# A planner for TensorE's order that counts changes of matmul shape and tends to keep a shape, with the remainders of the MLP's first level put last

## The chip, the core and the metric

The kernel runs on one NeuronCore of a Trainium2 chip. The metric is device time in microseconds (us) of the whole program, as the median of several runs. A profile of one execution stands beside it; its span runs from the first to the last instruction.

## The reference

Two blocks follow each other. The first is a recurrence over 768 steps for 4 batches and 8 heads, with a state of 40 x 40 for each:

```python
for t in range(S):
    y[:, :, t] = np.einsum('bhd,bhde->bhe', rt, state)
    Sa = np.einsum('bhde,bhe->bhd', state, at)
    state_decay = state * wt[:, :, None, :] - np.einsum('bhd,bhe->bhde', Sa, bt)
    state = state_decay + np.einsum('bhd,bhe->bhde', vt, kt)
```

Its output, brought into the form of 3072 tokens x 320, goes through an MLP with a hidden width of 2048, all in fp32:

```python
h = x @ w_in
g = h * (1.0 / (1.0 + np.exp(-h)))
return (g @ w_out).astype(np.float32)
```

## The kernel before

**The work.** The 768 steps are cut into 12 chunks of 64. Within a chunk the recurrence becomes matrix products: products between the scaled keys and the a vectors (between(), L560), the inverse of a unit triangular 64 x 64 matrix for each of 32 problems, a solve, and reads and updates of the state. Each chunk's output of 320 x 256 is then the input of the MLP for its 256 tokens.

For chunk n the following steps run, each written as a planned operation on one engine:

- load(n) and load_r(n) issue DMAs on SP: the decay w into wz, then b and k into kbv, a, v into vu, r and v transposed.
- prepare(n): VectorE scans the decays down and up (L505, L523), POOL (VectorE for n < 4) multiplies b and k into kb (L542) and scales a (L532). TensorE makes the products with b and with k (L560), the product with v (sv, L621) and two transposes of kb into kt (L646). ACT evicts (L633, L659, L285), VectorE masks (L606).
- special(n) for the chunks below NS = 4: a 16 x 16 inverse on VectorE with transfers through DRAM, and three steps on TensorE (L790, L803, L835, summed by VectorE in L850).
- inverse(k) for each pair of chunks from 4 on: the blocks of both chunks go through DRAM into mi, VectorE inverts 32 x 32 blocks (multiply L672, reduce L673), and DMAs bring the blocks into ZQ and X. merge(n) joins them with two groups of small matmuls (L915, L944).
- chain(n): the state is applied to a (right, L987, summed with R in L997), the solve (L1011) with its eviction into vu (L285, L289), its transposed form (solve_t, L1042), the transpose of the state G into GT (L1072), the update of the state (L1099, then L1115 on VectorE).
- read(n): products of r with v and u (look, L1141, masked in L1153) and then write(): the state's part (L1178) and the part of the chunk (L1191), both accumulated in one PSUM tile. VectorE scales it (L1202); it goes to DRAM (xh, L1219) and bring(n) fetches it as xt (L1259, L1261).
- moe(n): the MLP. The first level multiplies w_in by xt: 320 rows are two full tiles of 128 rows (full, L1271) and a remainder of 64 rows (rest, L1284), in which two row halves are used. Four rooms of 4 x 256 columns each are filled; the order is full(0), rest(0 and 1), full(1), then the same for 2 and 3. ACT applies the activation (gate, L1294). The second level (second, L1311) accumulates 16 matmuls with w_out for each of two halves of 128 tokens, VectorE copies the result (L1323) and SP sends it out.

**PSUM.** Four tiles called pair, of two banks each, hold all matmul results. A Room is a claim on one of them: it is taken by the first operation that names it and given back after a stated number of operations. Two more tiles, lam, in SBUF, are shared in the same way.

**The order.** No order is written out. Every step calls add(engine, cost, do, reads, writes, pri, rooms, k): the cost in us, a priority in which 10 stands for a chunk, and the number of instructions k that TensorE has to fetch. Plan.order() simulates five engines: for each engine it looks at the operations that are ready, takes those that can start within SLACK of the earliest (0.4 us for TensorE), and of these the one with the smallest priority. Among the engines it takes the operation that starts first. walk() models the fetching of TensorE's instructions in blocks of 256, and MOST and SHARE keep small matmuls (k over 32) and large ones (k of 32 or less) mixed. The operations are then issued in this order, which is fixed when the program is built: each engine works its queue in order and waits by semaphores. A cost in the planner changes no duration on the chip, only the order. `ahead()` lowers the priority value by 9 for the steps of chain, read and bring that are not on TensorE.

```python
least = min(x for _, x, _ in starts)
near = [x for x in starts if x[1] <= least + self.SLACK[e]]
if e == "PE" and mixed > self.MOST:
    near = [x for x in near if x[2]["k"] < 33] or near
s, _, op = min(near, key=lambda x: (x[2]["pri"], x[2]["n"]))
```

Of the kernel before, what the change touches and what calls it, by code (L numbers as in the profile page):

```python
# [32 lines left out]
class Plan:  # L33
# [8 lines left out]
    def add(self, engine, cost, do, r=(), w=(), pri=0, rooms=(), k=0, size=0.0, after=0.0):  # L42
        op = dict(
            engine=engine, cost=cost, do=do, pri=pri, rooms=rooms, k=k, size=size, n=len(self.ops), after=after
        )
# [21 lines left out]
    MOST, SHARE = 1.5, 2.0  # L67

# [24 lines left out]
    def order(self):  # L93
        ops = self.ops
        self.fetched, self.count = [0.0, 0.0], 0
# [9 lines left out]
        for op in ops:  # L105
            op["ready"] = op["after"]
        while len(out) < len(ops):
            best = None
            for e, some in ready.items():
                starts = []  # L110
                for op in some:
# [7 lines left out]
                    if e == "PE" and s < 1e8:  # L119
                        lost = self.walk(s, op["cost"], op["k"]) - s - op["cost"]  # L120
# [7 lines left out]
                s, _, op = min(near, key=lambda x: (x[2]["pri"], x[2]["n"]))  # L128
# [8 lines left out]
            at[e] = end = self.walk(s, op["cost"], op["k"], True) if e == "PE" else s + op["cost"]  # L137
# [29 lines left out]
def kernel(  # L167
# [171 lines left out]
    def weights(n):  # L339
# [42 lines left out]
        for h in range(2):  # L382
            for i in (1, 0):
# [10 lines left out]
                add("PE", 0.97, sum_, me, [(pf, h)], pri, [pf], 2)  # L394
# [93 lines left out]
    def prepare(n):  # L488
# [80 lines left out]
        add("PE", 1.14, partial(between, 1, pb_), ["B", ("a", i3)], [pb_, ("sb", i2)], pri, [pb_], 128)  # L569
# [17 lines left out]
        else:  # L587
            for b in range(2):
                for c in range(2):
                    q0 = 64 * i2 + 32 * c + 16 * b  # L590
                    r0 = 64 * b + 32 * c
                    dma(
                        lambda q0=q0, r0=r0, c=c: nc.sync.dma_start(
                            md[n // 2 % 2][q0 : q0 + 16].rearrange("q s t -> s q t"),
# [4 lines left out]
                        [("md", n // 2 % 2, i2, b, c)],  # L599
# [3 lines left out]
        add("PE", 1.14, partial(between, 0, pk), ["K", ("a", i3)], [pk], pri + 0.5, [pk, sk], 128)  # L603
# [25 lines left out]
        add("PE", 1.14, sv, [sk, ("v", i2, 0), ("v", i2, 1)], [pv, ("R", i3)], pri + 0.6, [pv, sk], 128)  # L629
# [9 lines left out]
        for b in range(2):  # L639
# [15 lines left out]
            add("PE", 0.75, turn, ["K", "B"], [pt, ("kt", i3, b)], pri + 0.7, [pt], 33)  # L655
# [76 lines left out]
    def special(n):  # L732
# [82 lines left out]
        for part in parts:  # L815
            XI_, X_ = keyed(("XI",), part), keyed(("X2", i2), part)
            k = len(part)
            add("PE", 0.57 * k, partial(both, pm[part], lambda b, g: S_[half(b), g, :], block, part), [("sb", i2), *mik], [pm[part], *XI_], pri, [pm[part]], 64 * k)
            add("PE", 0.3 * k, partial(turn, pd[part], part), mik, [pd[part]], pri, [pd[part]], 16 * k)
# [706 lines left out]
```

## Time and profile before

| what | value |
|---|---|
| median of 3 runs | 751.06 us (749.36 to 753.55) |
| the profiled execution | 748.01 us, with a span of 746.2 us |
| mean granted TensorE clock | 0.987 |
| VectorE / ACT / POOL busy | 53% / 26% / 11% of the span |
| first matmul | 13.71 us after the start |
| mean share of DMA engines, moved | 75.72 MB in the span |

The page's groups name a line, an engine, an operation, output and inputs, the shape and the count; then busy time, mean duration in ns, and the idle time of the engine just ahead of it with the releaser. PE is TensorE's matmul, PEld its weight load, which overlaps it. An fp32 matmul appears as two passes, so that 32 matmuls of one planned operation give 64 entries. The ends of matmuls are modelled and overlap the next start; the time of a group is therefore taken here from its start to the start of the group after it.

### The profile page before, as it was taken

To read this page: it belongs to the slowest core of one execution; us is meant where nothing else is said; L and a number is where in the kernel's file an instruction comes from. 1 tells how busy PE (TensorE), PEld (TensorE's weight loads), DVE (VectorE), ACT (ScalarE), POOL (GpSimd) and SP (SyncE) were. 2 spreads that over 40 slices of the span, in tenths; PEclk is the share of its full clock that TensorE was granted. 3 is DMA by queue.
4 is the path that set the end of the run, shared out by engine and by line. 5 is a ranking of instruction groups with operands and counts; after the bars stand their busy time and mean duration, and the time that the engine had idled before them with its cause. 6 is when DMAs were issued, how large, how long until landed. Compare 5 with 4: busy or idle time off the path is not lost.

```text
span 746.2 us, 27622 instructions
## 1 busy us (share of the span) xinstructions
PE 680.2 (91%) x12810; PEld 538.4 (72%) x12810; DVE 397.0 (53%) x567; ACT 195.9 (26%) x240; POOL 81.9 (11%) x63
## 2 busy tenths in 40 slices
PE   2198998999979999999998999998999999999995
PEld 2176786687768777787776777776777878778773
DVE  6867889674624298245496344496354293320000
ACT  3264355032223113313213213213213203111010
POOL 3200000003004003103220013130013000000000
PEclk9999998999999999999999999999999999999999
DMA  7672833561532343354532344432341404121000
GB/s 246 154 231 74 273 123 94 155 183 19 144 88 87 96 124 79 92 136 125 135 94 70 64 121 131 133 94 66 69 117 44 111 18 87 42 63 40 18 1 22
DMA packets 116956, 75.72 MB, mean 101 GB/s; under 512 B 64546, under 2 KB 113634, under 8 KB 116194
## 3 DMA queue, kind: packets, MB, share of 16 engines
q1 hardware_dynamic: 112328, 63.10, 32.1%
q0 software_dynamic: 2096, 10.49, 4.0%
q8 instruction: 102, 1.67, 1.0%
q10 hardware_dynamic: 2410, 0.30, 0.3%
q14 instruction: 20, 0.16, 0.1%
HBM read 59.64 MB, written 13.83 MB: 98 GB/s over the span
## 4 chain that ended last, share of the span: by engine, by line
PE 64%; DVE 19%; DMA 6%; issue 3%; SPq 2%; ACT 2%; POOL 2%; ACTq 1%; DVEq 0%; POOLq 0%
PE pair L1311 21%; PE pair L1271 15%; DVE XI L672 6%; PE pair L1284 4%; DVE XI L673 4%; DMA wz<-in_wT 3%; PE pair L835 3%; PE pair L1141 3%; PE pair L1191 3%; DVE kbv L505 2%; PE pair L560 2%; PE pair L1099 2%; DVE wz L523 2%; POOL kb L542 2%; PE pair L1178 2%
## 5 line engine op out<-in xcount | busy, mean ns | idle before, releaser
L1311 PE MATMUL pair<-wo,gts 128*128 128x320 f32 x768 | 225.2, 445 | 2.5 <-ACT kt L659 2.5
L1311 PEld LDWEIGHTS pair<-wo,gts 128*128 128x128 f32 x768 | 143.6, 192 | 59.2 <-ACT kt L659 2.7
L1271 PE MATMUL pair<-xt,wi 128*128 128x256 f32 x768 | 179.5, 388 | 4.4 <-DMA xt<-xh 2.3
L1271 PEld LDWEIGHTS pair<-xt,wi 128*128 128x128 f32 x768 | 144.2, 192 | 29.5 <-issue 4.0
L1294 ACT ACTIVATE gts<-pair 128x1024 f32<-128x1024 f32 x48 | 49.1, 1023 | 178.2 <-PE pair L1271 92.1
L542 POOL TENSOR_TENSOR kb<-kbv 128x512 f32<-128x512 f32 (+1 forms) x24 | 48.3, 2028 | 321.8 <-DVE wc L512 220.6
L560 PE MATMUL pair<-a,kb 40*64 40x64 f32 x1536 | 30.2, 236 | 28.8 <-DVE a L532 28.8
L560 PEld LDWEIGHTS pair<-a,kb 40*64 40x64 f32 x1536 | 27.5, 149 | 34.0 <-issue 18.6
L1284 PE MATMUL pair<-xt,wi 64*128 64x256 f32 x384 | 48.9, 391 | 3.0 <-DVE ot L1323 2.0
L1323 DVE COPY ot<-pair 128x320 f32<-128x320 f32 x24 | 11.7, 488 | 70.5 <-PE pair L1311 70.5
L673 DVE TENSOR_REDUCE XI<-XI 128x64 f32<-128x512 f32 (+9 forms) x68 | 46.9, 690 | 2.3
L1284 PEld LDWEIGHTS pair<-xt,wi 64*128 64x128 f32 x384 | 35.0, 186 | 12.2 <-issue 5.4
L1153 DVE TENSOR_TENSOR lam<-pair,ml 128x1024 f32<-128x1024 f32 x24 | 29.0, 1219 | 23.8 <-PE pair L1141 23.8
L672 DVE TENSOR_TENSOR XI<-XI,mi 128x1024 f32<-128x1024 f32 (+8 forms) x48 | 36.2, 754 | 5.8 <-DMA mi<-md 4.7
L1202 DVE TENSOR_TENSOR lam<-pair,wz 128x1024 f32<-128x1024 f32 (+1 forms) x13 | 14.8, 1142 | 45.9 <-PE pair L1191 45.7
L523 DVE TENSOR_TENSOR_SCAN wz<-wz,zt 128x1024 f32<-128x1024 f32 x12 | 31.6, 2631 | 0.4
L1141 PEld LDWEIGHTS pair<-r,vut 40*64 40x64 f32 x1536 | 24.8, 135 | 6.1 <-issue 5.6
L606 DVE TENSOR_TENSOR lam<-pair,ml 128x1024 f32<-128x1024 f32 x12 | 14.6, 1219 | 27.2 <-PE pair L560 23.9
L1141 PE MATMUL pair<-r,vut 40*64 40x64 f32 x1536 | 27.9, 221 | 0.9 <-issue 0.9
L505 DVE TENSOR_TENSOR_SCAN kbv<-wz,zt 128x1024 f32<-128x1024 f32 x12 | 27.5, 2291 | 1.0
L1085 ACT COPY GT<-pair 128x640 f32<-128x640 f32 x11 | 7.6, 692 | 75.1 <-PE pair L1072 75.1
L285 ACT ACTIVATE sb<-pair 128x1024 f32<-128x1024 f32 x12 | 12.3, 1023 | 56.8 <-PE pair L560 56.8
(146 smaller groups left out, 725.9 us busy)
## 6 DMA issues: line engine op xcount, KB each, us to landing
wz<-in_wT SPq DMA_DIRECT2D x12, 512.0 KB, 5.2
kbv<-in_bT SPq DMA_DIRECT2D x12, 512.0 KB, 3.7
a<-in_aT SPq DMA_DIRECT2D x12, 512.0 KB, 5.3
kbv<-in_kT SPq DMA_DIRECT2D x12, 512.0 KB, 4.8
r<-in_rT SPq DMA_DIRECT2D x48, 96.0 KB, 2.6
vut<-in_vT SPq DMA_DIRECT2D x48, 96.0 KB, 3.1
vu<-in_v SPq DMA_DIRECT2D x24, 160.0 KB, 4.0
out<-ot SPq DMA_DIRECT2D x48, 80.0 KB, 2.0
```

The source lines that it names most:

```text
L505: nc.vector.tensor_tensor_scan(back(V), back(W[:, 2 : 2 + Q * C]), zt, 1.0, ALU.mult, ALU.add)
L523: nc.vector.tensor_tensor_scan(Z, Z, zt, 0.0, ALU.mult, ALU.add)
L542: TTn[engine].tensor_tensor(out=at_(kb, place(is_b, first), (576 * step, 4 // step), (128, 4), (1, C)), in0=blocks((kf, bf)[is_b]), in1=bl ...
L560: nc.tensor.matmul(room.tile[half(b), j, g * C : g * C + C], lhsT=kb[rows(j), place(is_b, q) : place(is_b, q) + C], rhs=A[rows(j), q * C : ...
L672: nc.vector.tensor_tensor(out=at_(tmp, 0, *dims), in0=x, in1=y, op=ALU.mult)
L673: nc.vector.tensor_reduce(out=out_, in_=at_(tmp, 0, *dims), axis=AX.X, op=ALU.add)
L1141: nc.tensor.matmul(pl.tile[half(1 - b if role else b), b, c * C : c * C + C], lhsT=vut[rows(b), role, hu, :], rhs=rs[rows(b), hh, :], star ...
L1153: lambda pl=pl, la=la: nc.vector.tensor_tensor(out=la.tile.rearrange("p (q t) -> p q t", q=Q), in0=pl.tile.rearrange("p a b -> p (a b)").r ...
L1271: nc.tensor.matmul(rooms[g].tile[:, f // 2, (f % 2) * T : (f % 2) * T + T], lhsT=wi[:, k, (4 * g + f) * 128 : (4 * g + f) * 128 + 128], rh ...
L1284: nc.tensor.matmul(rooms[g].tile[:, h, (f % 2) * T : (f % 2) * T + T], lhsT=wi3[half(h), g * 256 + (f % 2) * 128 : g * 256 + (f % 2) * 128 ...
L1294: nc.scalar.activation(out=gts[:, 4 * g * T : 4 * g * T + 4 * T], in_=rooms[g].tile.rearrange("p a b -> p (a b)"), func=AF.Silu)
L1311: nc.tensor.matmul(po[b].tile[:, 0, 0:DM], lhsT=g4[:, f, 128 * b : 128 * b + 128], rhs=wo[:, f, :], start=f == 0, stop=f == NF - 1,)
```

## The change

The planner gets a shape for each operation of TensorE: F for whole-array matmuls, R for the remainder, T for transposes, H for products over 128 rows with 40 columns of weights, S for 32 x 32 tiles, and Q, the default, for 64 x 64 tiles. turn() returns a time for going from one shape to another, which is added ahead of an operation. Of the candidates within the slack, one with the present shape has its priority value lowered by BONUS = 4. TensorE's costs are set anew, without the change of shape in them, and k falls from 33 to 32 for the transposes. The argument `after` of add() goes; it was 0.0 everywhere.

```diff
+    LEAVE = {"F": 0.09, "R": 0.2, "T": 0.13, "Q": 0.13, "H": 0.12, "S": 0.11}
+    ENTER = {"F": 0.08, "R": 0.1, "T": 0.03, "Q": 0.03, "H": 0.03, "S": 0.03}
+    BONUS = 4
+
+    def turn(self, op):
+
+        a, b = self.shape, op["shape"]
+        if a == b or {a, b} == {"R", "T"}:
+            return 0.03 if a != "F" else 0.0
+        return self.LEAVE[a] + self.ENTER[b]
...
-                        lost = self.walk(s, op["cost"], op["k"]) - s - op["cost"]
+                        lost = self.walk(s + self.turn(op), op["cost"], op["k"]) - s - op["cost"]
...
-                s, _, op = min(near, key=lambda x: (x[2]["pri"], x[2]["n"]))
+                s, _, op = min(near, key=lambda x: (x[2]["pri"] - self.BONUS * (e == "PE" and x[2]["shape"] == self.shape), x[2]["n"]))
...
-            at[e] = end = self.walk(s, op["cost"], op["k"], True) if e == "PE" else s + op["cost"]
+                at[e] = end = self.walk(s + self.turn(op), op["cost"], op["k"], True)
+                self.shape = op["shape"]
+            else:
+                at[e] = end = s + op["cost"]
```

The costs, by example:

```diff
-        add("PE", 1.14, partial(between, 1, pb_), ["B", ("a", i3)], [pb_, ("sb", i2)], pri, [pb_], 128)
+        add("PE", 0.9, partial(between, 1, pb_), ["B", ("a", i3)], [pb_, ("sb", i2)], pri, [pb_], 128)
...
-            add("PE", 0.75, turn, ["K", "B"], [pt, ("kt", i3, b)], pri + 0.7, [pt], 33)
+            add("PE", 0.5, turn, ["K", "B"], [pt, ("kt", i3, b)], pri + 0.7, [pt], 32, shape="T")
```

In read(), the state's part of the write becomes an operation of its own. It may stand long before the other part, and the PSUM pair is then held from it on:

```diff
-            cost = 3.05 if n else 0.95 * len(part)
-            add("PE", cost, partial(write, part, py_[part]), ktk + rk + used + (["GT"] if n else []), [py_[part]], pri, [py_[part], *used], 256 if n else 64 * len(part))
+            if n:
+                add("PE", 0.9, partial(write_state, py_[part]), [*rk, "GT"], [py_[part]], pri, [py_[part]], 128)
+            add("PE", 0.87 * len(part), partial(write, part, py_[part]), ktk + used, [py_[part]], pri, [py_[part], *used], 64 * len(part), shape="H")
```

In moe(), both full operations come first, and the remainder of both rooms after them; the accumulation starts in the full ones and ends in the remainder. The second level no longer names the last gate as its input:

```diff
-            add("PE", 3.6, partial(full, g), [*xk[0], *xk[1], *w_(g)], [a_, ("gts", g), ("gts", g + 1)], pri + g, [a_], 32)
-            add("PE", 2.0, partial(rest, g), [*xk[2], *xk[3], ("wi3",)], [a_, b_], pri + g + 0.1, [a_, b_], 32)
-            add("PE", 3.6, partial(full, g + 1), [*xk[0], *xk[1], *w_(g + 1)], [b_], pri + g + 0.2, [b_], 32)
+            for i, x in enumerate((a_, b_)):
+                add("PE", 3.45, partial(full, g + i), [*xk[0], *xk[1], *w_(g + i)], [x, ("ff", n), ("gts", g + i)], pri + g + 0.1 * i, [x], 32, shape="F")
+            add("PE", 1.72, partial(rest, g), [*xk[2], *xk[3], ("wi3",)], [a_, b_], pri + g + 0.2, [a_, b_], 32, shape="R")
...
-                add("PE", 2.17, partial(second, b, part), [("gts", part), ("gts", 3), *need], [po[b]], pri + 4 + b + part * 0.1, [po[b]], 16)
+                add("PE", 2.14, partial(second, b, part), [("gts", part), *need], [po[b]], pri + 4 + b + part * 0.1, [po[b]], 16, shape="F")
```

special(), inverse(), merge() and the loop that calls them count pairs of chunks from NS on instead of from 0; with NS = 4 the buffers and priorities that result are the same numbers.

## The prediction

> **What bounds it now.** Line numbers are those of the kernel before. I read the page first (span, busy times, groups), then TensorE's waits, the chain of waits, the timeline, and last the order in which TensorE's groups stand in the two built programs, which holds no times.
>
> ```profile
> span 746.2 us, 27622 instructions
> ...
> PE 680.2 (91%) x12810; PEld 538.4 (72%) x12810; DVE 397.0 (53%) x567; ACT 195.9 (26%) x240; POOL 81.9 (11%) x63
> ...
> L1311 PE MATMUL pair<-wo,gts 128*128 128x320 f32 x768 | 225.2, 445 | 2.5 <-ACT kt L659 2.5
> L1271 PE MATMUL pair<-xt,wi 128*128 128x256 f32 x768 | 179.5, 388 | 4.4 <-DMA xt<-xh 2.3
> ```
>
> TensorE is busy 91% of the span: 66 us are left, 13.7 ahead of the first matmul and 8.3 after the last MLP matmul at 738.0. So the time falls either because TensorE's groups take less, or because the remaining 44 us of stalls shrink. TensorE's waits (us in total, times, longest) say who ends them:
>
> ```profile
> PE pair L560 <- DVE a L532: 28.8, 2, 15.1
> PE pair L835 <- DVE XI L850: 4.2, 1, 4.2
> PE pair L915 <- DMA ZQ<-zd: 3.4, 4, 1.4
> PE pair L1011 <- DVE R L997: 2.3, 2, 1.7
> ```
>
> 28.8 us belong to the two waits of the start, which the change does not touch. The others lie on the recurrence. Two rates hide in the chain of waits (start, us, what); the x counts passes, two for each fp32 matmul:
>
> ```profile
> 589.88 2.35 PE pair L1311 x8
> 592.23 1.07 PE pair L621 x64
> ...
> 593.92 15.27 PE pair L1311 x56
> ```
>
> Eight passes of L1311 alone take 2.35 us; 56 in one run take 15.27, or 2.15 each eight plus 0.2 once. Leaving and re-entering the whole-array shape therefore costs 0.2 us. L1271 says the same: 3.65 for 16 passes alone, 7.10 for 32 ("616.37 7.10"), so 0.2 is saved. The timeline gives it for small matmuls:
>
> ```profile
> 348.65 2.10 PE L1141 MATMUL pair<-r,vut 40*64 40x64 f32 x128
> 350.68 3.72 PE L1271 MATMUL pair<-xt,wi 128*128 128x256 f32 x16
> ...
> 461.75 1.16 PE L1141 MATMUL pair<-r,vut 40*64 40x64 f32 x64
> 462.84 3.72 PE L1271 MATMUL pair<-xt,wi 128*128 128x256 f32 x16
> ```
>
> From start to next start, 128 passes take 2.03 us and 64 take 1.09: joining two small groups saves 0.15 (0.11 where their lines differ: L1011 ahead of L1042 takes 0.955, its like L987 ahead of a transpose 1.07). The chain of waits also shows the longest fixed path of the middle, from the write of an odd chunk to the merge of the next even one:
>
> ```profile
> 467.60 1.94 PE pair L1191 x64
> ...
> 471.56 5.42 DMA wz<-in_wT
> ...
> 482.68 2.29 DVE wz L523
> ...
> 514.03 1.23 DVE XI L673
> ...
> 515.29 1.99 ACT mi L878
> ...
> 517.74 2.69 DMA ZQ<-zd
> ...
> 520.57 0.22 PE pair L915 x2
> ```
>
> From the end of L1191 (469.5) to L915 (520.6) it takes 51.1 us, whatever TensorE does: the decay tile of the next chunk is loaded, scanned, inverted in blocks on VectorE and sent through DRAM.
>
> [...] The page has 102 instruction packets with 1.67 MB on one queue, 16 KB each; whether they hide in long stretches of small matmuls is open, see below. [...] after the 2.1 us stall ahead of 70.37, a group of L1271 took 5.41 us instead of 3.65. So a long stall may cost twice.
>
> **Part by part.** (1) New costs and turn(), the bonus of 4 and the split write remove no instruction; both programs have the same matmuls. Counted in the order of TensorE, neighbours of different shape fall from 286 to 227, exits from whole-array work (L1271, L1311, L386) from 98 to 64, and neighbours that both work in 64x64 tiles rise from 21 to 38 with like lines joined. 34 x 0.197 = 6.7 us, 17 x 0.11 = 1.9: 8.6 us less of TensorE's running time. Priced group by group with such start-to-start times, the order of before sums to 657.9 and that of after to 649.1, 8.8 less. No other engine hides this, since TensorE sets the end; it is lost only where TensorE then waits.
>
> (2) Where groups moved. I cut at L915 of chunks 4, 6, 8, 10 (296.5, 408.2, 520.6, 629.0) and at the end of L1191 of chunks 5, 7, 9 (357.3, 469.5, 581.5). From L915 to the odd write, before took 60.8, 61.3 and 60.9, of which its priced groups are 55.4, 58.0 and 58.0. After, priced groups there sum to 49.8, 53.8 and 49.8. The last, for instance: one half of L1271 (3.65), one remainder L1284 (1.93), one L560 (1.09), two L646 (1.24) and one L1178 (1.03) move behind the odd write; L987 and L1072 (1.60) come in; four exits are gone (0.8): 8.1. So the odd write, which starts the 51 us path, comes earlier; the moved groups fill time in which TensorE had waited for L915.
>
> (3) Stalls there. VectorE's order puts the scans L505 and L523 behind the odd chunk's L997, L289 and L1115, so the 1.7 us wait of L1011 goes. What is late next is a tight row of small groups. From L1191 of the even chunk to the next L1271, 1,088 instructions (each matmul two passes, each with its weight load) stand with no large matmul between, three times; before had such rows only in the start. The one to judge by:
>
> ```profile
> 56.79 1.52 PE L1141 MATMUL pair<-r,vut 40*64 40x64 f32 x80
> ...
> 59.22 0.93 PE L1141 MATMUL pair<-r,vut 40*64 40x64 f32 x48 [0.92 <-issue]
> ```
>
> These 256 instructions took 3.29 us instead of 2.03. If each block beyond two costs such 1.26, a row costs (1088 - 512) / 256 x 1.26 = 2.8; the other end is nothing, since elsewhere 256 in 2.03 passed without a stall. The hops in the row (VectorE 0.81 plus 0.3 against covers of 1.0) add 0.1 each, at the same places. I take 2.5 for each segment, 0 to 5. Queued behind a stalled small group is all of TensorE; the MLP's input hides it, because from the end of L1191 it takes about 8.3 us until xt has landed (1.3 for L1202, 3.5 until xt is issued at 438.82, 3.4 to landing), against a cover of 8.65 in the new order. On SP, xt of chunks 4 and 8 now stands behind the load of vu, which waits for L1099 of the odd chunk: about 0.3 us late at worst, inside the 2.5.
>
> (4) From the odd write to L915, before took 50.9, 51.1 and 47.5 (priced 47.2, 47.1, 47.2; the last has no load of wz). After, the priced groups are 47.8, 54.1 and 49.3. I take the longer of path and groups: 51, 54.1 + 1.0 and 49.3 + 0.5, the additions for hand-overs of PSUM (5). From 629.0 to 738.0 before took 109.0; after, 109.0 + 0.7.
>
> (5) Remainders (L1284) last, and the state's part of the write split off (L1178): the room of L1178 is held from its early start until the write, 43 us of priced groups for chunk 4. Three of the four pairs remain. Where a full half follows a remainder into the same pair, it needs 0.11 + 1.02 (L1294) + 0.06 = 1.19 us, and is covered by one remainder of 0.96: 0.23 us, at some four places. That is in the 0.5 to 1.0 above.
>
> (6) The new indices of inverse() and merge() give the same numbers for NS = 4: nothing. The removed key ("gts", 3) only frees the planner.
>
> (7) The first 296.5 us hold 236.5 of groups before and 235.5 after; VectorE and the weights set them. I carry over its stalls: 296, between 288 (VectorE's work ahead of chunk 1's write, priced by its instructions, falls from 115.9 to 106.2) and 304 (two more waits such as the 4.2 of L835).
>
> The sum: 296 + 52.3 + 51 + 56.3 + 55.1 + 52.3 + 49.8 + 109.7 + 8.3 = 730.8, against 746.2: 15.4 us less. The profiled execution took 748.01, 1.8 beyond its span, and the median of the runs shown is 751.06; on that scale 751.06 - 15.4 = 735.7.
>
> **Rivals.** Stalls only move: the running time falls by 8.7 and the dense rows eat what the earlier odd write brings: 742.4. For it: 2.8 us for each row is possible; against: the scans are out of the chain. The odd write comes no earlier, because loads and POOL's L542 and L532 (6.8 + 2.4 us) set it, and TensorE's gain turns into waits: 749. The start gains too, by the 8 us that VectorE's order allows: 727. Slower: the held pair. In five stretches (chunks 2, 4, 6, 8, 10) some 22 groups each pass through three pairs; with 0.25 us for each hand-over, 110 x 0.25 = 27 us, or 763. It decides the sign from 19 us on, 0.17 for each. Against it: most successive groups there use different pairs, with over 1.2 us between. That the change does not do what it says is excluded by the counted order.
>
> **Numbers.** Forecast 0.50, own range 728 to 744; stalls only move 0.20; no earlier 0.10; the start gains 0.12; slower 0.08. Within 0.5% (747.3 to 754.8) is about what a measurement of this kernel can tell from no change. Faster 0.82, same 0.10, slower 0.08. The range, 725 to 751, reaches to the gaining start and to the late write.
>
> **What would show it.** Right: TensorE's busy time near 671; L1311 in fewer and longer runs; no wait of L1011 for L997 above 0.5 us; under 54 us from L915 to the odd write; small stalls by "issue" in the dense rows. Wrong: L915 waiting over 4 us for ZQ (the path is longer than 51), waits of L1271 or L1141 for ACT or VectorE in the stretches with the held pair, or L915 of chunk 4 later than 304.

## The result and the profile after

The changed kernel takes 777.07 us (median of 4 runs, 774.32 to 778.14) against 750.78 us for the kernel before on the same chip (median of 4, 749.36 to 753.55): a ratio of 1.034, 95% interval 1.030 to 1.038. It is slower by 26 us where 15 us less were forecast. The profiled execution took 778.14 us and is the slowest of the four; that of before took 748.01, less than the four of before, so the two spans lie 30.2 us apart and the medians 26.3. Executions over 1.5% above the fastest of their kernel (2 of 30 of before in one series, 4 of 11 of joined below, its profiled one among them) count in no ratio. Lines of code have moved by 13 to 17: L1328 is the second level (was L1311), L1288 the full tiles of the first (L1271), L1301 the remainder (L1284), L573 between() (L560), L849 more() (L835), L930 the first group of merge() (L915), L1026 the solve (L1011), L1156 look (L1141), L1207 the write (L1191), L1192 its state part (L1178), L660 the transposes of kb (L646), L1057 solve_t (L1042), L1114 the update (L1099), L1340 the copy of the MLP's result (L1323).

The page of the kernel after, with the span, the busy times, the granted clock in tenths over 40 slices, and the two MLP groups:

```profile
span 776.4 us, 27607 instructions
...
PE 698.6 (90%) x12810; PEld 562.2 (72%) x12810; DVE 398.3 (51%) x567; ACT 193.2 (25%) x240; POOL 79.3 (10%) x63
...
PEclk9999999998999979998998996999897999999998
...
L1328 PE MATMUL pair<-wo,gts 128*128 128x320 f32 x768 | 224.8, 449 | 1.3 <-ACT kt L673 1.3
...
L1288 PE MATMUL pair<-xt,wi 128*128 128x256 f32 x768 | 185.0, 401 | 1.3 <-DVE XI L864 0.8
```

TensorE issues the same 12,810 matmul passes, yet is busy 698.6 us instead of 680.2. Its mean granted clock fell from 0.987 to 0.944 (0.952 to 0.959 in the other three executions). In the clock row 8 of the 40 digits are 6 to 8, spread over the whole program. TensorE's waits (us in total, times, longest):

```profile
PE pair L573 <- DVE a L545: 28.9, 2, 15.4
PE pair L849 <- DVE XI L864: 7.8, 3, 3.1
PE pair L660 <- DVE ot L1340: 5.0, 1, 5.0
PE pair L1156 <- issue: 4.7, 4, 1.6
...
PE pair L930 <- DMA ZQ<-zd: 0.7, 1, 0.7
```

The start (L573) is as before, L930 waits less, and the solve's wait for the sum R (2.3 us before: L1011 for L997) is gone, as forecast. Waits named "issue", in which nothing that the profile shows was missing, grow from 4.9 us in 6 to 16.6 in 15. All 15 stand inside a group of equal matmuls, and each ends 2.2 to 2.8 us after a packet on the DMA queue that the page calls "instruction" (q8, 102 packets for 25,620 matmul passes and weight loads, so 251 for each) has started.

I made an account of both spans from the traces. Each group of TensorE is priced at its undisturbed start-to-start time, as in the prediction; what it took beyond that is put to idle time (by its releaser), to stretches in which the granted clock was 0.5, or to the rest:

| us | before | after | difference |
|---|---|---|---|
| priced groups | 657.7 | 649.1 | -8.6 |
| idle, "issue" | 4.9 | 16.6 | +11.7 |
| idle, waits for another engine or a DMA | 39.3 | 39.9 | +0.6 |
| lost at half clock (half of TensorE's busy time in it) | 7.6 | 36.4 | +28.8 |
| rest, time ahead of the first matmul and after the last | 36.8 | 34.5 | -2.3 |
| span (sums are rounded) | 746.2 | 776.4 | +30.2 |

The priced groups are the prediction's own prices applied to the built order, so their 8.6 us repeat its sum and measure nothing. What the trace can tell is the first row and the last together: they fell from 694.5 us to 683.6, by 10.9, so a saving of about the forecast size came. The loss is in two rows: issue stalls and half clock. Of their 40.5 us, 11.7 are the issue stalls themselves, 18.2 the half clock that follows issue stalls (none before), and 10.5 more half clock behind waits for data. The clock was at half for 89 us, before for 22, both counted to the end of the last clock record, some 2 us past the span.

The sum of the waits for data hides a move: up to L930 of chunk 4 they rose from 27.2 to 34.0 us, from there to the last L930 they fell from 12.0 to 5.1.

The second dense row of the kernel after, from its timeline (start, us, engine, line, count, idle before):

```profile
464.69 0.41 PE L1057 MATMUL pair<-X,R 64*40 64x64 f32 x14
468.07 1.65 PE L1057 MATMUL pair<-X,R 64*40 64x64 f32 x50 [2.97 <-issue]
...
471.94 3.79 PE L1156 MATMUL pair<-r,vut 40*64 40x64 f32 x128
...
476.89 9.21 PE L1288 MATMUL pair<-xt,wi 128*128 128x256 f32 x32
```

A group whose operands lay ready stopped after 14 of its 64 passes for 2.97 us. What follows it is slow, though nothing waits: 128 passes of L1156 take 3.79 us where 2.10 were shown of before, 32 of L1288 take 9.21 where 7.10 were. The windows view of the same place (window, length, busy time of PE, PEld, DVE, ACT, POOL, granted clock, DMA share, GB/s):

```profile
460.57:463.99 3.42, 3.40 (x180) 3.09 (x178) 2.05 (x2) 0.69 (x1) 0.00 (x0) 1.00 0.54 132
463.99:467.40 3.41, 1.11 (x77) 0.95 (x69) 0.82 (x1) 0.70 (x1) 0.00 (x0) 1.00 0.86 220
467.40:470.81 3.41, 2.74 (x86) 2.58 (x87) 0.00 (x0) 0.99 (x1) 0.00 (x0) 0.50 0.80 266
...
481.05:484.47 3.42, 3.42 (x18) 3.01 (x17) 3.39 (x3) 0.00 (x0) 3.42 (x3) 1.00 0.11 11
```

The stall leaves one window of 3.41 us with 1.11 us of work. From its end the clock is 0.50, for four windows, until whole-array work has filled one. (A window here is a stretch of 3.41 us between the times at which the clock changes.) So the stall of 2.97 us cost 6.2 us more, by the account.

### The profile page after: what moved, and what is told of

The parts are those of the page before. It is cut to its first block, busy times and chain, and to the rows that moved or that the text cites. A ratio compares the mean times of both kernels' runs of the same rounds, so it can differ in the third digit from the quotient of the medians.

```text
span 776.4 us, 27607 instructions
## 1 busy us (share of the span) xinstructions
PE 698.6 (90%) x12810; PEld 562.2 (72%) x12810; DVE 398.3 (51%) x567; ACT 193.2 (25%) x240; POOL 79.3 (10%) x63
## 3 DMA queue, kind: packets, MB, share of 16 engines
q8 instruction: 102, 1.67, 0.9%
## 4 chain that ended last, share of the span: by engine, by line
PE 69%; DVE 16%; issue 5%; DMA 5%; ACT 3%; SPq 2%; ACTq 0%; DVEq 0%
PE pair L1328 23%; PE pair L1288 18%; PE pair L1301 4%; DVE XI L686 4%; DMA wz<-in_wT 4%; PE pair L1156 3%; PE pair L1207 3%; DVE wz L536 2%; PE pair L573 2%; PE pair L849 2%; PE pair L1114 2%; DVE kbv L518 2%; DVE XI L687 2%; PE pair L1002 1%; PE pair L1192 1%
## 5 line engine op out<-in xcount | busy, mean ns | idle before, releaser
L1328 PE MATMUL pair<-wo,gts 128*128 128x320 f32 x768 | 224.8, 449 | 1.3 <-ACT kt L673 1.3
L1328 PEld LDWEIGHTS pair<-wo,gts 128*128 128x128 f32 x768 | 146.6, 195 | 61.5 <-issue 4.9
L1288 PE MATMUL pair<-xt,wi 128*128 128x256 f32 x768 | 185.0, 401 | 1.3 <-DVE XI L864 0.8
L1288 PEld LDWEIGHTS pair<-xt,wi 128*128 128x128 f32 x768 | 153.1, 202 | 27.4 <-ACT gts L1311 1.3
L1311 ACT ACTIVATE gts<-pair 128x1024 f32<-128x1024 f32 x48 | 46.7, 1021 | 156.5 <-PE pair L1301 156.4
L555 POOL TENSOR_TENSOR kb<-kbv 128x512 f32<-128x512 f32 (+1 forms) x24 | 44.1, 1858 | 396.3 <-DVE kbv L518 197.1
L573 PE MATMUL pair<-a,kb 40*64 40x64 f32 x1536 | 29.9, 232 | 30.5 <-DVE a L545 28.9
L573 PEld LDWEIGHTS pair<-a,kb 40*64 40x64 f32 x1536 | 27.0, 146 | 33.4 <-issue 17.0
L1168 DVE TENSOR_TENSOR lam<-pair,ml 128x1024 f32<-128x1024 f32 x24 | 29.2, 1222 | 41.0 <-PE pair L1156 41.0
L1301 PE MATMUL pair<-xt,wi 64*128 64x256 f32 x384 | 49.0, 396 | 0.0
L1340 DVE COPY ot<-pair 128x320 f32<-128x320 f32 x24 | 11.7, 488 | 69.8 <-PE pair L1328 67.1
L1301 PEld LDWEIGHTS pair<-xt,wi 64*128 64x128 f32 x384 | 35.9, 191 | 7.1 <-issue 2.3
L1156 PE MATMUL pair<-r,vut 40*64 40x64 f32 x1536 | 30.0, 228 | 4.7 <-issue 4.7
L1156 PEld LDWEIGHTS pair<-r,vut 40*64 40x64 f32 x1536 | 26.6, 142 | 8.9 <-issue 8.0
L849 PE MATMUL pair<-XI 64*64 64x64 f32 x512 | 20.2, 241 | 8.7 <-DVE XI L864 7.8
L849 PEld LDWEIGHTS pair<-XI 64*64 64x64 f32 x512 | 18.8, 154 | 12.1 <-DVE XI L864 9.1
```

What stands on the lines that cost most here:

```text
L555: TTn[engine].tensor_tensor(out=at_(kb, place(is_b, first), (576 * step, 4 // step), (128, 4), (1, C)), in0=blocks((kf, bf)[is_b]), in1=bl ...
L573: nc.tensor.matmul(room.tile[half(b), j, g * C : g * C + C], lhsT=kb[rows(j), place(is_b, q) : place(is_b, q) + C], rhs=A[rows(j), q * C : ...
L849: nc.tensor.matmul(py.tile[half(x), b, q * C : q * C + C], lhsT=MT[half(x), c], rhs=src[half(x), c], start=True, stop=True,)
L1156: nc.tensor.matmul(pl.tile[half(1 - b if role else b), b, c * C : c * C + C], lhsT=vut[rows(b), role, hu, :], rhs=rs[rows(b), hh, :], star ...
L1288: nc.tensor.matmul(rooms[g].tile[:, f // 2, (f % 2) * T : (f % 2) * T + T], lhsT=wi[:, k, (4 * g + f) * 128 : (4 * g + f) * 128 + 128], rh ...
L1301: nc.tensor.matmul(rooms[g].tile[:, h, (f % 2) * T : (f % 2) * T + T], lhsT=wi3[half(h), g * 256 + (f % 2) * 128 : g * 256 + (f % 2) * 128 ...
```

## Theories

A: long rows of small matmuls without whole-array work outrun the supply of instructions; the stall that follows halves the clock. B: the PSUM pair held by the split write causes waits. C: keeping a shape costs the clock as such. D, formed after the first four runs: any new order moves the waits for data, by amounts that no sum of the prediction held.

For A, the orders of the built programs were counted: rows of over 512 instructions without whole-array work or remainder. Before has 2 (1216 and 864, both in the start), after 6 (1248, 1088 three times, 992, 576).

## Experiments

All ratios are against the kernel before, run on the same chip. The table has the account of the profiled execution of each kernel, made as above ("half clock" is what was lost at it); of joined only the times are used. A profiled execution can lie several us from its kernel's median (mixF_most2 777.88, bonus0 767.73, mixF 763.02), so differences of a few us between rows mean little. Of the issue column, 8.7 us of k32_alone and 4.1 of k33_bonus2 stand between two groups and are, by the timeline, waits for data for which the trace names nobody.

| kernel | median us | ratio (95%) | priced | issue | data | half clock |
|---|---|---|---|---|---|---|
| k33 | 747.45 | 0.996 (0.994 to 0.998) | 651.3 | 4.1 | 38.1 | 15.0 |
| joined | 747.35 | 0.997 (0.994 to 1.001) | | | | |
| k32_alone | 756.28 | 1.011 (1.004 to 1.017) | 656.5 | 13.1 | 32.9 | 18.4 |
| after_most1 | 759.09 | 1.011 (1.005 to 1.017) | 651.2 | 9.5 | 48.6 | 13.0 |
| bonus0 | 762.91 | 1.017 (1.014 to 1.020) | 655.2 | 11.9 | 39.0 | 20.9 |
| k33_most2 | 764.13 | 1.019 (1.014 to 1.024) | 648.0 | 10.0 | 51.3 | 17.3 |
| k33_bonus2 | 764.71 | 1.020 (1.016 to 1.024) | 653.5 | 12.3 | 43.7 | 21.4 |
| rest_last | 766.05 | 1.021 (1.017 to 1.025) | 655.3 | 10.4 | 45.1 | 18.9 |
| mixF | 766.66 | 1.028 (1.021 to 1.035) | 647.4 | 19.3 | 31.8 | 27.2 |
| mixF_most2 | 769.52 | 1.028 (1.022 to 1.034) | 647.9 | 10.6 | 54.0 | 25.3 |
| dense12 | 772.87 | 1.030 (1.026 to 1.035) | 668.2 | 10.0 | 39.7 | 20.2 |
| warm2 | 774.94 | 1.037 (1.032 to 1.043) | 653.6 | 16.0 | 40.8 | 21.4 |

The added matmuls of warm2 are only partly in its priced groups; its rest is some 6 us above that of after.

**k33: two numbers of the change undone.**

```diff
-            add("PE", 0.5, turn, ["K", "B"], [pt, ("kt", i3, b)], pri + 0.7, [pt], 32, shape="T")
+            add("PE", 0.5, turn, ["K", "B"], [pt, ("kt", i3, b)], pri + 0.7, [pt], 33, shape="T")
...
-            add("PE", 0.5, turn, ["G"], [pt, "GT"], pri + 0.3, [pt], 32, shape="T")
+            add("PE", 0.5, turn, ["G"], [pt, "GT"], pri + 0.3, [pt], 33, shape="T")
```

> The changed kernel with one number undone: the transposes count 33 instructions again instead of 32, so that the planner's rule on mixing takes them for small matmuls. Theory A (long rows of small matmuls outrun the instruction fetch, and their stalls halve TensorE's clock): only 2 rows of more than 512 instructions without a large matmul remain, both in the start, as in the kernel before (6 in the changed one), the clock is low for under 35 us, and the time is 740 to 752. Theory B (the pair of PSUM held by the split write causes the waits, and these the low clock): the split is still there, so 770 to 778. Theory C (keeping a shape costs the clock, in rows of any length): exits from large matmuls are 80 against 98 before and 64 after, so about half of the loss, 760 to 766.

Measured 747.45 us: A's range, 30 us below after and 0.4% below before. B and C, which had 770 to 778 and 760 to 766, are excluded as the whole cause. The clock was low for 41 us, though, where A had said under 35. The planner's rule `mixed > MOST` asks for operations with k below 33 after 1.5 us of small work, and such operations lower the count. At 32 a transpose, which is small work, counts as large. At 33 the three dense rows are gone, and so are the issue stalls (16.6 to 4.1) and most of the half clock (36.4 to 15.0). The same steps in the timeline of k33:

```profile
446.17 3.72 PE L1288 MATMUL pair<-xt,wi 128*128 128x256 f32 x16
449.82 1.43 PE L1114 MATMUL pair<-vu,kt 128*40 128x40 f32 x64
...
454.14 2.19 PE L1156 MATMUL pair<-r,vut 40*64 40x64 f32 x128
456.26 7.17 PE L1288 MATMUL pair<-xt,wi 128*128 128x256 f32 x32
```

L1288 stands between the small groups; L1156 takes 2.19 us again and 32 passes of L1288 take 7.17.

**dense12: only the length of a row.** In the kernel before, the first look group of chunk 5 is issued 12 times over.

```diff
-                for o in problems("j", "z", "x", "role", "b"):
+                for o in problems("j", "z", "x", "role", "b") * (12 if n == 5 and m == 0 else 1):
```

> The kernel before, with the first of the two groups of L1141 of chunk 5 issued 12 times in a row instead of once, into the same PSUM tile with the same results; 1,408 instructions of small matmuls are added, which need nothing new from any other engine, and are worth 11.2 us at the pace of an undisturbed group (64 passes in 1.02). Theory A (instruction supply): the 12 groups (1,536 instructions) take 18 us or more, every 256 instructions beyond the first blocks taking over 3.5 us instead of 2.03, with gaps inside groups that nothing else explains, and half clock after them; the whole 763 to 775. If small matmuls are supplied at their pace: 12 to 13 us, no half clock, and the whole 760 to 764. As the supply of instructions is here the only resource that changes, the length of that stretch decides, not the sum.

```profile
350.71 3.24 PE L1141 MATMUL pair<-r,vut 40*64 40x64 f32 x203
355.21 2.52 PE L1141 MATMUL pair<-r,vut 40*64 40x64 f32 x128 [1.26 <-issue]
358.94 14.12 PE L1141 MATMUL pair<-r,vut 40*64 40x64 f32 x501 [1.21 <-issue]
372.99 1.22 PE L1271 MATMUL pair<-xt,wi 128*128 128x256 f32 x2
```

The clock and the DMA queues in that place, from the windows view and from the DMA view of 352 to 371 (in 40 slices):

```profile
356.67:377.15 20.48, 19.23 (x555) 17.93 (x548) 2.45 (x2) 0.00 (x0) 0.00 (x0) 0.50 0.08 24
...
DMA  0100000001000000100000001000000010000001
...
q8 instruction: 6, 0.10, 2.3%
```

The 832 passes (the 12 groups and the one after them) took 22.28 us, at 2.03 for 128 they are worth 13.2. The first 406 instructions (203 passes with their weight loads) run at pace. Then come two stalls in the midst of equal matmuls, and from 356.7 the clock is at half for 20.5 us. The whole took 772.87 us, A's range. The packets of the queue that the page calls "instruction" start at 352.5, 356.3, 360.1, 363.8, 367.2 and 370.7: one every 3.4 to 3.8 us, with nothing else on the DMA queues, and the two stalls stand 128 passes with their loads, 256 instructions, apart, while 256 small ones run in 2.03. So at full clock the supply is the limit; at half clock 256 instructions take 3.6 us (501 passes with their loads in 14.12), as long as the packets' interval, so that no gap is seen any more. Of the 9.1 us that the row took too long, 2.5 are the two stalls, and most of the rest is half clock. This is the case that decides for A's mechanism, since nothing but the row's length was changed.

**k32_alone and rest_last: two parts of the change by themselves, in the kernel before.** k32_alone has only the diff of k33 the other way round (33 to 32, with the old costs). rest_last has only the new order of full tiles and remainders, with the old costs 3.6, 3.6 and 2.0.

> The kernel before with one edit: the two kinds of transposes (L646, L1072) are declared with k = 32 where it has 33, so that the planner counts them as large work when it mixes small and large. Nothing else of the change is in it. In its order rows of over 512 instructions without whole-array work rise from 2 to 8 (1248, 800, 736, 704 three times, 576 twice). Theory A (long rows of small matmuls wait for their instructions, and the clock is halved in the window after such a wait): slower than before, 758 to 768 us, with TensorE at half clock for 40 us or more against 22. Theory D, formed from the run with the remainders alone (the loss sits in waits for data of groups moved against each other, of which the number 33 is only one cause): 748 to 753, since the costs and priorities stay those of before.

> The kernel before with one part of the change alone: the remainders of the first MLP level come after both full halves. Costs, priorities and mixing are those of before. A: one more row of 1184 instructions than before, so 748 to 756. B and C: 746 to 751, nothing is held and no shape is preferred.

k32_alone took 756.28 us: slower, with 45 us of half clock, but 2 us less than A's range, and above D's. Its longest stall that is called "issue" is none of supply:

```profile
565.63 0.81 DVE L997 TENSOR_TENSOR R<-pair,R 128x640 f32<-128x640 f32 x1
...
566.55 1.95 PE L1011 MATMUL pair<-R,X 64*64 64x40 f32 x64 [5.70 <-issue]
```

VectorE's L997, which L1011 needs, had only ended at 566.4; it stood in VectorE's queue behind the small L1380, which had waited for ACT's L554 until 564.9. Two more such waits of L1011 are of this kind (2.45 and 0.54 us), so that only some 4 us of its 13.1 are supply. That it came near A's range is therefore mostly luck, and no evidence for A. rest_last took 766.05, which neither theory had: mine were 746 to 756. Of its rows only one is new (1184); two stalls of 1.55 and 1.56 us stand in it, and issue waits are 5.5 us more than before in all. Waits for data are 5.8 us more, the longest new ones these:

```profile
PE pair L835 <- DVE XI L850: 5.7, 1, 5.7
PE pair L646 <- DVE R L997: 4.4, 1, 4.4
```

This made D necessary. A part that is worth nothing by itself in my sum cost 16 us, through waits of both kinds in other places and the half clock behind them (18.9 us, 7.6 before).

**joined and bonus0: two more parts taken back out of the kernel after.** joined makes one operation of the write again:

```diff
+            def whole(part=part):
+                if n:
+                    write_state(py_[part])
+                write(part, py_[part])
...
+            add("PE", cost, whole, ktk + rk + used + (["GT"] if n else []), [py_[part]], pri, [py_[part], *used], 256 if n else 64 * len(part), shape="H")
```

bonus0 has `BONUS = 0`.

> The changed kernel with the state's part of the write joined to the other part again, so that no pair of PSUM is held early. Rows of over 512 instructions: 11, the eight new ones of 576, just over two blocks. A: most of the long stalls go, small ones stay: 752 to 765. B: all of the loss goes and the gain of running time shows: 738 to 748. C: switches are as few as in the changed kernel, so no gain, 772 to 778.

> The changed kernel with BONUS = 0: changes of shape still cost time in the planner, but no shape is preferred. Rows of over 512 instructions without a large matmul: 7, the middle ones of 704 instead of 1088. A: part of the loss goes, 757 to 768. B: the split write stays, 770 to 778. C: switches are 268 of 286, so nearly all of the loss goes, 750 to 755.

joined took 747.35 us, 30 below after: in B's range, and 5 below A's. That speaks for the split write as a part of the cause, but k33 ran as fast with the split in place, and without the split the three rows of 1,088 go too (joined has 1248, 992, 704 and eight of 576), and the waits in after that are named by a reader of a pair (the longest 5.0 us) come nowhere near 30 us in sum. The two theories are not told apart by this run. bonus0 took 762.91, in A's range; C is out, since with no bonus left the kernel is still 12.6 us slower than before (762.91 against 750.3).

**after_most1, mixF, mixF_most2: the mixing rule turned.** after_most1 has MOST = 1.0. mixF decides by shape, and mixF_most2 is the same with MOST = 2.0:

```diff
-                    near = [x for x in near if x[2]["k"] < 33] or near
+                    near = [x for x in near if x[2]["shape"] in "FR"] or near
...
-                mixed = mixed + op["cost"] if op["k"] > 32 else max(0.0, mixed - self.SHARE * op["cost"])
+                mixed = mixed + op["cost"] if op["shape"] not in "FR" else max(0.0, mixed - self.SHARE * op["cost"])
```

> The kernel after with one constant of the planner changed: MOST is 1.0 instead of 1.5, so that it turns to whole-array work after 1.0 us of work counted as small instead of 1.5. Rows of over 512 instructions without whole-array work fall from 6 to 4 (1248, 1056, 576, 576), the planner's own price of the changes rises by 1.6 us. Theory A: most of the loss comes back, 748 to 760 us, half clock below 50 us against 89. Theory C (keeping a shape costs the clock, however the rows are cut): 770 to 778.

> The kernel after with the planner's mixing decided by shape: only work of the whole array (shapes F and R) lowers the count of small work and is asked for when the count passes 1.5, the transposes no longer. That corrects the rule that I suspected; but the order that comes of it has even longer rows: 2752, 1312, 1088, 1088, 1056, 672 and 640 instructions, with the lowest price of shape changes of all (624.2 on a scale where after is 626.2). Theory A: the rows decide, whatever the rule: 770 us or more, with half clock and issue stalls in the three rows of the middle, the one of 2,752 above all. If the rule decides by something else than rows: 745 to 755.

> The kernel before this one in the list with MOST at 2.0 instead of 1.5: the same rule, but in its order only two rows of over 512 instructions remain (1312 and 1056, both in the first tenth of the program). Theory A: issue stalls and half-clock loss after the start near those of the kernel before (some 4 and 8 to 15 us), and with waits for data like those of before, 740 to 750 us; where it is slower than that, the excess must be in waits for data.

after_most1 took 759.09, in A's range: half clock fell to 37 us and its loss by 23.4, issue by 7.1; but the waits for data rose by 8.7. mixF took 766.66, 3.3 below A's bound and far above the rival's. Its three rows in the middle hold 10.9 of its 19.3 us of issue stalls, and each row has 10.2 us of half clock behind a stall (the longest are 2.69 us ahead of L1192 at 349.76 and 2.67 at 576.72), so the rows weigh more than the rule as such; the waits for data fell by 8.1, which A had not in its sum. mixF_most2 removes these rows and takes 769.52. A's range was missed by 20 us. The excess is, as its expectation said it had to be, in waits for data (54.0 us, 14.7 above before) and the half clock behind them, but not there alone: issue stalls are 5.7 us above before, and 7.4 us of them stand in rows of 256 to 384 instructions, which a count of rows over 512 leaves out.

**warm2: whole-array work put into the dense rows.**

```diff
+                if n in (5, 7, 9):
+                    for _ in range(8):
+                        nc.tensor.matmul(pg.tile[:, 0, 0:256], lhsT=wi[:, 0, 0:128], rhs=wi[:, 0, 0:256], start=True, stop=True)
```

> The kernel after, with eight whole-array matmuls (16 passes of 128 rows by 256 columns, worth 3.65 us and 0.2 for leaving them) added ahead of the update L1114 of chunks 5, 7 and 9, in the middle of the three dense rows; they write the PSUM tile that the update overwrites, so the results stay, and the order of all else is the same. Work added: 3 x 3.85 = 11.6 us. Theory A (supply of instructions, and the half clock after it): the row is cut in two, some 7 us of issue stalls and 20 us or more of half-clock loss go, the whole is faster in spite of the added work: 755 to 768 us. Theories B and C (the loss is spread over waits on PSUM or comes with keeping a shape): 785 to 790.

Measured 774.94 us, 2 below after, with 11.6 us of work added; beside the kernel before that ran with each it is 27.8 above, and after was 26.3 above. So some 10 to 14 us came back, which B and C exclude, but A's range was missed by 7. The half-clock loss fell by 15.0, the issue stalls by 0.6 in all instead of 7. The second row shows why:

```profile
466.42 0.25 PE L1026 MATMUL pair<-R,X 64*64 64x40 f32 x1 [2.01 <-issue]
...
467.49 3.72 PE L1113 MATMUL pair<-wi 128*128 128x256 f32 x16
...
475.94 7.17 PE L1291 MATMUL pair<-xt,wi 128*128 128x256 f32 x32
```

A stall of 2.01 us still comes ahead of the added work (L1113), because the part of the row ahead of L1113 is already 672 instructions. But the clock stays at 1.00, and L1291 takes 7.17 instead of 9.21. The stall is spread over two windows: the first has 1.27 us of idle time and no whole-array work, the second 0.80 and 1.55 us of L1113. So L1113 can have saved the second window, but not the first, which was not followed by half clock although of 189 windows with as little whole-array work and at least 0.65 us of idle 103 were (the last section has the count). From the start of the even chunk's write to L1291 this row took 17.2 us with 3.85 us of added work, and 17.8 without.

**k33_most2 and k33_bonus2: is there a version below both?** k33 with MOST = 2.0, and k33 with BONUS = 2.

> The kernel after with the transposes' k back at 33 and MOST at 2.0: a candidate that may beat both kernels. Its rows of over 512 instructions are 1216 and 1120 (as with k at 33 alone), the planner's price of the changes is 2.1 us lower than that run's. Theory A: 743 to 748 us, half clock near 40 us. Theory D (waits for data between groups that have been moved): anything from 744 to 760, without a tie to the rows.

> The kernel after with the transposes' k back at 33 and the bonus for keeping a shape at 2 instead of 4: the last candidate for a version below both kernels, near the run with k at 33 alone. Its rows of over 512 instructions are 1216 and 1120, both in the start, and one of 672; the planner's price of the changes is 1.7 us above that run's. Theory A, with what the runs so far showed (every stretch of 3.41 us with 0.5 us or more of idle TensorE and little whole-array work is followed by half clock, 1.7 us for each 3.41): 746 to 753 us if its waits for data stay near 23 us. Theory D (each new order moves the waits for data by up to 14 us): up to 765, with the excess in waits for data and the half clock behind them, and not in issue stalls.

764.13 and 764.71 us: 16 and 12 above A's ranges, the first also 4 above D's, the second just inside it. Their rows are nearly those of k33, but the waits for data are 51.3 and 43.7 us instead of 38.1, and issue and half clock rise with them. In k33_bonus2 two of 4.9 and 4.6 us stand ahead of L1288, for VectorE's L302 in both:

```profile
PE pair L1288 <- DVE vu L302: 9.5, 2, 4.9
```

In k33_most2, 5.5 us of issue stalls stand in seven rows of 384 instructions, so here too A's count of rows over 512 is too coarse; in k33_bonus2 two of 2.0 and 1.7 stand in its row of 672. And the rule in k33_bonus2's expectation, that every such stretch is followed by half clock, is too strong: of 189 with at least 0.65 us of idle 86 were not (the last section has the count). k33, 0.4% below before, and joined stay the best orders that were run.

Not tried: the dense rows of after cut by moving one real group of L1328 into them, with all else in place. The PSUM pair that it would hold longer is taken by a group within the row, so that this would have been another order.

## Why the prediction was wrong, step by step

The profiled span is 45.6 us above the forecast 730.8. By its own cuts (start-to-start, us):

| stretch | forecast | measured |
|---|---|---|
| to L930 of chunk 4 (step 7) | 296 | 311.1 |
| to the odd writes (steps 2, 3) | 52.3, 56.3, 52.3 | 58.1, 64.0, 63.3 |
| odd write to L930 (step 4) | 51, 55.1, 49.8 | 54.7, 55.5, 49.6 |
| last L930 to the last MLP matmul | 109.7 | 112.1 |

Step 1 was right in kind, and in size as far as the account can tell: 10.9 us less of running time and rest, where 8.6 were forecast.

Step 2 was right for the groups (51.7, 53.1 and 49.1 priced against 49.8, 53.8 and 49.8), so the odd write could have come earlier. The waits for data of the middle did fall, by 6.9 us.

Step 3 is the step that failed. It saw the rows and the issue stalls and took 2.5 us each, 5 at most. From the even write to the next L1288 the rows took 16.5, 17.8 and 16.6 us for 10.6 of priced groups: 5.9 to 7.2 each, and the L1288 behind them 1.4, 2.0 and 2.7 more. The third row:

```profile
578.42 1.99 PE L1207 MATMUL pair<-lam,kt 128*40 128x64 f32 x64
...
591.30 1.07 PE L1192 MATMUL pair<-r,GT 40*40 40x64 f32 x27 [2.12 <-issue]
...
595.03 9.87 PE L1288 MATMUL pair<-xt,wi 128*128 128x256 f32 x32
```

Two terms were off, the first a little and the second wholly. The stalls themselves are 3.3, 3.1 and 3.7 us for a row, where 2.8 were worked out and 2.5 taken: a block beyond the first two was charged 1.26 us, from the row in the start of before, while in the third row, with the clock still at 1, packets came 4.3 us apart (580.3, 584.6, 588.9) against 2.03 of use. And the clock behind a stall was left at 1, at no cost: the odd-write stretches hold 17 us lost at half clock (3.0, 6.2 and 7.8, of the last some 3 from a stall ahead of its row).

The sentence "a long stall may cost twice" stood in the prediction and no number followed from it. That is the largest term of the miss: +28.8 us, of the 36.4 in after, 18.2 lie behind issue stalls (before: none) and 18.1 behind waits for data (before: 7.6), though these waits are in sum no longer than before. The longest is step 5's hand-over at a place that I had not priced: the transposes L660 waited 4.97 us for a PSUM pair that VectorE had still to copy out, behind the blocks of inverse() in its queue.

```profile
285.54 0.48 DVE L1340 COPY ot<-pair 128x320 f32<-128x320 f32 x1
...
286.17 1.93 PE L660 MATMUL pair<-ident,kb 40*128 40x40 f32 x32 [4.97 <-DVE ot L1340]
```

The clock went to half 3.1 us before that wait ended and stayed there for 10.2 us. Step 5's "0.23 us at four places" fails there; its rival of 110 hand-overs at 0.25 us is wrong as well, since the waits are few and long; that rival had the sign right, for a reason of which the trace shows only a small part.

Step 7 carried the start over, with 304 as its limit. It is 15.1 us longer, a third of the whole miss: 9 lost at half clock and 8 more idle (6.8 of them waits for data), with some 2 less of running groups. Which move made the waits there longer was not tried. VectorE's lighter load ahead of chunk 1's write brought nothing that can be seen.

Step 4 held: 3.7 us off in the first (3.3 of them half clock), 0.4 and 0.2 in the others. The path through the decay tile is 49.6 to 55.5 us, as read.

And one thing was named but never followed: "k falls from 33 to 32" stands in the list of changes, with the rule beside it. What the planner then does with a transpose could have been read in its code, and k33 shows that these two numbers decide the sign here. They do so through the order that comes of them: alone, in the kernel before, they cost 6 us, not 30.

What stays open. The runs show the mechanism (dense12), its removal (k33) and its partial removal (warm2, after_most1). They don't allow a sum over the parts: rest_last and k32_alone cost 16 and 6 us alone, taking back the numbers or the split write gains 30 each. Each part yields another order, and the orders that I ran lie between 747 and 777 us with priced groups of 647 to 658 (dense12, with its added work, left out). Nor was it tried why the packets come later in the rows of after than in dense12; in the second row the DMA share is 0.54 to 0.86 ahead of the stall and in it, and in dense12 at most 0.08.

## What to carry to other kernels

Price the clock with the stall: where a row of small matmuls is broken by a wait of a microsecond, allow for half-clock windows behind it (in after four behind the stall of 2.97 us, for 6.2 us), and ask what whole-array work stands close enough to prevent them (over 1.4 us of it in the window of the wait was enough in 71 of 71). Count, in the built order, the rows of instructions without large work before trusting any saving per instruction. Rows beyond two blocks of 256 were broken by the supply again and again here (12 of the 15 stalls of after stand in five of its six such rows), but shorter ones can be too: the other 3 stand in rows of 256 to 416. In a list-scheduled kernel a constant is also a threshold for every rule that reads it, and a saving of 1% is less than what a new order moves in waits: try several orders and keep the best.

## What the runs showed of the hardware

The supply of instructions. The packets of the queue q8 have 16 KB each (102 with 1.67 MB in after). Issue stalls that follow each other in a row of after stand 250 to 256 passes and weight loads apart (six times) or 512 (once), those of dense12 256: a packet goes with 256 instructions. Large matmuls hardly ever wait so. In the 14 traces 133 issue stalls stand inside a group of equal matmuls, 128 of them in small ones (5 in L1271, L1288 or L1284), and 132 end 2.16 to 2.92 us after a packet starts; of all passes of after, 13% start at such a distance. No two of these packets start closer than 3.10 us, while small fp32 matmuls use 256 instructions up in 2.03. So a long row of them did not keep its pace: the 832 passes of dense12 took 22.28 us instead of 13.2, half clock included.

The clock. In the traces the granted clock is 0.5 or 1, and between two changes lies a multiple of 3.41 us (in after 3.41 to 13.65 at half and 17.07 to 105.81 at full). Less than a microsecond of idle time in a window of small work was followed by half clock too: in before 0.73 us, in the window from 111.75. Over 13 profiled executions (joined left out), in windows between the first and the last matmul and with remainders counted as whole-array work, I count 105 falls to half clock. All came after a window with at most 1.32 us of whole-array work; 103 of these windows had at least 0.65 us of idle, the least 0.34. Of 71 windows with at least 0.5 us idle but over 1.4 us of whole-array work, none was followed by half clock. The reverse doesn't hold: of 189 windows at full clock with at most 1.32 us of whole-array work and at least 0.65 us idle, 103 were followed by half clock and 86 were not; with 2 us idle or more, all 41 were. What decides between the two was not found.

A window at half clock costs up to 1.7 us in the account, 1.5 on average in after (36.4 us in 24 windows). Small matmuls alone seldom end it: after 34 of 44 half-clock windows without whole-array work the clock stayed low, after 9 of 91 with 2 us or more of it.
